# All slot sums on VectorE, and the dense blocks' weights split a pair of blocks ahead

## The chip, the cores and the metric

The kernel runs on one core of a Trainium2 chip. The metric is the time of one execution on the device in microseconds (us); several runs are taken, and their median is compared. The engines are TensorE (PE in the profile, with PEld for its weight loads), VectorE (DVE), ScalarE (ACT), GpSimd (POOL) and SyncE (SP), which issues most transfers. Each engine works through its own queue in order.

## What is computed

One layer, on 2048 tokens of width 512: `x + attention(xn) + experts(xn)`, where `xn` is the layer norm of `x`.

```python
# attention: 32 heads of 16, one shared key and value head
p = softmax(einsum("bhqd,bkd->bhqk", q, k) * Dh ** -0.5)
o = einsum("bhqk,bkd->bhqd", p, v) -> (B, S, 512) @ wo
# experts: 4096 of them, product keys 64 x 64, 32 heads, 2 experts per head and token
s1, s2 = q1 @ k1.T, q2 @ k2.T            # 64 scores each
top 2 of s1, top 2 of s2 -> 4 candidates -> top 2: expert e, gate g = softmax
act = gelu(xn . u[e]);  out = sum over 32 heads, 2 experts of g * act * v[e]
```

## The kernel before, in words

**Two ways for the experts.** The 16 token tiles of 128 form four groups. For groups 0 and 1 the experts are gathered: a *slot* is one expert for each token of a tile, 64 slots per tile, 512 in all. A slot's steps are: an indirect DMA on GpSimd's queue brings 128 rows of u and v (`gather`, L728) into one of 9 buffers (`NGB`); VectorE multiplies u with xn and sums up (`dot`, L740); for each four slots ScalarE makes the tanh of the gelu (`tanh`, L751) and VectorE the weights w (L762, L763); last, the *slot sum* adds w * v to the tile's accumulator (`add`, from L754). Of four slots, VectorE sums three with one instruction each (L772). The fourth is scaled by ScalarE (L769) and added by GpSimd (L770); `adds` (L790) puts it into the list `LATE`, which runs later in the step.

For groups 2 and 3 all 4096 experts are computed, in 32 *blocks* of 128 (`dense`, L558). Before the blocks, *one-hot* batches turn gates and indices into a table of gates (L608 to L636: VectorE L612, L614, L615, TensorE L629). A block's weights come from DRAM (`fetch`, L565, two buffers) and are split into a high and a low part for three-term products (`split`, L584: ScalarE copies the high part, L589, GpSimd subtracts it, L590, once for u and once for v). The parts go into `wk` buffers, of which there are eight (`NWK`); a block takes two. TensorE then makes 12 matmuls (`pact`, L674), ScalarE and VectorE form the gated activations (L692 to L702), and after each odd block `sums` (L646) multiplies the pair of blocks before with its v parts (L656), which VectorE adds up (L659). Block b's gates come by `fetch_gates` (L574).

**The order of the work.** It is written out by hand; each engine's instructions stand in the order in which the program emits them. The main loop makes 256 attention steps and 24 more (`att_steps`, L861). A step emits: the transfers put off in `STORES`; score matmuls (L312) with two exps on ScalarE (L315); the products of the step before's exps with the values (L326); `mid` (L955: tanhs, the activations put off in `ON_ACT` and `BEHIND`, up to four `adds`); two more scores with exps; `LATE`; up to four gathers; and a *filler*. Ahead of each step come as many dots as the count `pos` asks for: 1.65 a step, 2.4 in dense stages.

The filler takes pieces of one long thread (`score_thread`, L834): the experts' scores and top 2 (*items*, L453 to L465) of all groups, and behind group 2's and group 3's items their one-hot batches and dense blocks. Each piece yields its cost in units (`UNIT` for a matmul), and `FILL` sets how many units the loop spends by its last step, the same share in each. At the start of the loop 16.7 units are spent. So the stages are, in this order: items, one-hot, dense blocks, items, one-hot, dense blocks, tail.

Of the kernel before, what the change touches and what calls it, by code (L numbers as in the profile page):

```python
# [16 lines left out]
AF = mybir.ActivationFunctionType  # L17
OP = mybir.AluOpType
# [23 lines left out]
NWK = 8  # L42
NIDX = 10
GS = 8192.0
FILL = 925.0
SCALE = DH ** -0.5
LIMIT2 = 25000.0
C_IN = 0.7978845608028654
C_CUB = 0.044715 * C_IN
POOL_EACH = 4  # L50
UNIT = 0.235


# [1 line left out]
def tile_kernel(ctx, tc, x, wq, wkv, wo, wqT, kT, uv, ub, vb, out):  # L55
    nc = tc.nc
# [47 lines left out]
    for j in range(4):  # L104
        v = blk_f[:, 8 * j:8 * j + 8]
# [452 lines left out]
    def dense(DG, after):  # L558
# [6 lines left out]
        def fetch(b):  # L565
            if b < NB and b not in raws:
                rw = big.tile([P, 2, 512], F32, name="rw", tag="wqt", bufs=2)
                nc.sync.dma_start(rw[:, 0, :], ub[b])
                nc.sync.dma_start(rw[:, 1, :], vb[b])
                raws[b] = rw  # L570
# [13 lines left out]
        def split(b):  # L584
            if b < NB:
                rw = raws.pop(b)
                us, vs = wk_tile(), wk_tile()
                for i, w in enumerate((us, vs)):
                    nc.scalar.copy(w[:, 0, :], rw[:, i, :])  # L589
                    nc.gpsimd.tensor_tensor(out=w[:, 1, :], in0=rw[:, i, :], in1=w[:, 0, :], op=OP.subtract)  # L590
                splits[b] = us, vs
# [29 lines left out]
        for q in range(512 // TB):  # L621
            t0, ql = q // 4 * 64, q % 4
            if ql == 0:
                st = [late[0].tile([P, 16, 64], F32, name="gst", tag="wd", bufs=4) for _ in range(2)]
            onehot(q + 1)
            oa, ob = OH.pop(q)
            p = xtile("pg")
            for i in range(TB):
                nc.tensor.matmul(p[:, i * NB:(i + 1) * NB], oa[:, :, i], ob[:, :, i], start=True, stop=True)  # L629
            pv_ = p.rearrange("p (t b) -> p b t", b=NB)  # L630
            for hb in range(2):
                nc.scalar.copy(st[hb][:, :, ql * TB:(ql + 1) * TB], pv_[:, 16 * hb:16 * hb + 16, :])
            if ql == 3:
                for hb in range(2):
                    store(lambda t0=t0, hb=hb, st=st: nc.sync.dma_start(
                        d_g[16 * hb:16 * hb + 16, :, t0:t0 + 64].rearrange("b p t -> p b t"), st[hb]))  # L636
            yield 1.4
        for j in range(2):
            da = big.tile([P, 2, D], F32, name="da", tag="da", bufs=2)
            for i in range(2):  # L640
# [21 lines left out]
        stt = nc.vector.scalar_tensor_tensor  # L662
        dense_on[0] = 1
        split(0)
        store(lambda: fetch(2))
        run(STORES)
        fetch_gates(0)
        for b in range(NB):
            us, vs = splits.pop(b)
            p = xtile("pact")  # L670
            n = 0
            for k in range(KC):
                for a, c in TERMS:
                    nc.tensor.matmul(p, us[:, a, k * P:(k + 1) * P], XT[DG][k][:, c, :],  # L674
                                     start=n == 0, stop=n == 11)
                    n += 1
                if k == 0:
                    split(b + 1)
                    store(lambda b=b: fetch(b + 3))
                    store(lambda b=b: fetch_gates(b + 1))  # L680
                if k == KC - 1 and b == NB - 1 and after is not None:
                    wp_read(after, range(2))
                if b == NB - 1 and after is not None:
                    load_phase2_xt(SEQ[after][0], k)
                if k < KC - 1:
                    yield 3 * UNIT
            wd = late[0].tile([P, 2, 512], F32R, name="wd", tag="wd", bufs=4)
            if b not in gates:
                run(STORES)
            gy = gates.pop(b)  # L690
            g, y = gy[:, 0, :], gy[:, 1, :]
            nc.scalar.activation(y, p, AF.Square, scale=C_CUB ** 0.5)  # L692
            stt(g, g, 1.0 / GS, p, op0=OP.mult, op1=OP.mult)  # L693
            stt(y, y, C_IN, p, op0=OP.add, op1=OP.mult)  # L694

            def gate(y=y, g=g, wd=wd):
                stt(wd[:, 0, :], y, 1.0, g, op0=OP.add, op1=OP.mult)
                stt(y, y, 1.0, g, op0=OP.add, op1=OP.mult)
                nc.vector.tensor_tensor(out=wd[:, 1, :], in0=y, in1=wd[:, 0, :], op=OP.subtract)
                formed[0] += 1  # L700

            on_act(lambda y=y: nc.scalar.activation(y, y, AF.Tanh))  # L702
            behind(gate)
            held.append((wd, vs))
            yield 3 * UNIT
            if b % 2:
                if ready:
                    yield from sums()
                ready, held = held, []
# [44 lines left out]
    def add(m):  # L754
        ph, c, ti, s = slots[m]
        n, i = divmod(m, SB)
        if i == 0:
            a, th = ACTS.pop(n), TH.pop(n)
            s0 = s
            ga = small.tile([P, SB], F32, name="ga", bufs=3)  # L760
            w = small.tile([P, SB], F32, name="w", bufs=3)
            nc.vector.tensor_mul(ga, a, G[ph, c, ti][:, s0:s0 + SB])  # L762
            nc.vector.scalar_tensor_tensor(w, th, 1.0, ga, op0=OP.add, op1=OP.mult)  # L763
            WT[n] = w
        w = WT[n]
        acc = ACC[TPH * ph + ti]
        v = UV.pop(m)[:, D:]
        if m % POOL_EACH == POOL_EACH - 1:
            nc.scalar.activation(v, v, AF.Copy, scale=w[:, i:i + 1])  # L769
            nc.gpsimd.tensor_tensor(out=acc, in0=acc, in1=v, op=OP.add)  # L770
        else:
            nc.vector.scalar_tensor_tensor(acc, v, w[:, i:i + 1], acc, op0=OP.mult, op1=OP.add)  # L772
        if c == NC - 1 and s == NEG - 1:
            experts_out(TPH * ph + ti)

# [13 lines left out]

    def adds(most):  # L790
        while a_next[0] < a_ready[0] and most > 0:
            m = a_next[0]
            if m % POOL_EACH == POOL_EACH - 1:
                LATE.append(lambda m=m: add(m))
            else:
                add(m)
            a_next[0] += 1
            most -= 1

# [3 lines left out]
            a_ready[0] += SB  # L803


    ON_ACT, BEHIND, LATE, STORES = [], [], [], []
    store = STORES.append
    on_act, behind = ON_ACT.append, BEHIND.append

    def run(fns):  # L810
        todo = fns[:]
        fns.clear()
        for fn in todo:
            fn()
# [44 lines left out]


    def att_steps(d, mid, fill):  # L861
        i = 2 * d
        run(STORES)
        if i < STEPS:
            u, kc = divmod(i, 16)
            if i == 0:
                load_q(0)
            if kc == 4 and u + 1 < 32:
                load_q(u + 1)
            scores(u, kc, 0)  # L870
            scores(u, kc, 1)
        if 0 < i <= STEPS:
            pu, pk = divmod(i - 2, 16)
            pv(pu, pk)
            pv(pu, pk + 1)
            if pk == 14:
                unit_tail(pu)
        mid()
        if i < STEPS:
            scores(u, kc + 1, 0)  # L880
            scores(u, kc + 1, 1)
        run(LATE)
        gathers(4)
        fill()

        if i >= 40 and (i - 40) % 32 == 0 and i - 40 < STEPS:
            pair_tail((i - 40) // 32)
        if i >= 144 and (i - 144) % 128 < 16 and i % 4 == 0:
            qb, j = (i - 144) // 128, (i - 144) % 128 // 4
            block_out(qb, j)  # L890
            spent[0] += 3.6
# [37 lines left out]
    for m in range(0, first, SB):  # L929
        dots(m + SB)  # L930
        tanhs(d_next[0])
        adds(SB)
        run(LATE)
        gathers(SB)
    run(STORES)
    start_stack.close()
# [5 lines left out]
    with tc.manual_schedule(engines={E_.PE, E_.Activation, E_.DVE, E_.Pool, E_.SP}):  # L942
        done0 = spent[0]
        half = STEPS // 2
        pos = float(first)
        for d in range(half + 24):

            if d < half * 3 // 4:
                pos += 2.4 if dense_on[0] else 1.65
            else:  # L950
                pos += max(0.0, NSL - pos) / max(half - 4 - d, 1)
            before = d_next[0]
            dots(int(pos + 0.001))

            def mid():  # L955
                tanhs(before)
                run(ON_ACT)
                run(BEHIND)
                adds(4)

            att_steps(d, mid, lambda: run_scores(until=done0 + (FILL - done0) * (d + 1) / half if d < half else 1e6))
        flush()
        run(STORES)
        while a_next[0] < NSL:
            dots(NSL)
            tanhs(d_next[0])
            adds(SB)
            run(LATE)
            run(STORES)
            gathers(NGB)  # L970
        run(STORES)
# [37 lines left out]
```

## Time and profile before

| | |
|---|---|
| median of 3 runs | 2504.38 us (2497.44 to 2505.39) |
| the profiled execution | 2493.88 us |
| its span, first to last instruction | 2492.2 us |
| mean granted TensorE clock | 0.892 of full speed |
| TensorE / VectorE / ScalarE / GpSimd busy | 83% / 74% / 54% / 35% |
| moved by DMA | 492 MB, 197 GB/s |

Busy shares are means over all stages, which have different limits; so a stage is read by itself, in a table of busy time over stretches of the span. In such a table each engine's busy time stands with its count of instructions (x), then the granted clock. In lists of waits, a row reads: engine and line that waited, `<-` who ended the wait, and then the total in us, the times, and the longest. In rows by group, after the bar: busy us, mean ns of one, idle us just before, and what ended most of it. In timelines: start, duration, engine, line and operation, and in brackets the idle time before it.

### The profile page before, as it was taken

The numbers are of one execution on the slowest core, as the hardware profiler recorded it, in microseconds if no ns is written. First come the engines' busy times: TensorE is split into PE (matmuls) and PEld (weight loads), VectorE is DVE, ScalarE is ACT, GpSimd is POOL, SyncE is SP. The second block draws the span as 40 slices with busy tenths as digits, with TensorE's granted clock in tenths as the row PEclk, the third lists the DMA queues.
The fourth block names the chain that finished last, engine by engine and source line by source line (L and its number), as shares of the span: only waits on it lengthen the run. The fifth ranks groups of instructions, "written<-read, shape, count | busy, mean of one in ns | idle before, by whom it ended". The sixth has DMA issues, their size and how long they took to land. (4 is left out here: it accounts for less than half of the span.)

```text
span 2492.2 us, 35439 instructions
## 1 busy us (share of the span) xinstructions
PE 2057.3 (83%) x10990; PEld 1080.3 (43%) x10990; DVE 1852.4 (74%) x6555; ACT 1346.9 (54%) x1830; POOL 877.5 (35%) x798
## 2 busy tenths in 40 slices
PE   5969898999967778877788899997877887877775
PEld 3624444555533444444444455554434344444431
DVE  5548687979985858877678579999758578777662
ACT  2346565655645665555555556564655565555552
POOL 2013222223223244545444333232234445444430
PEclk8979999999988889988888999998769889888887
DMA  5766666766635575556466677663675656555551
GB/s 191 278 227 220 212 235 224 257 223 218 232 120 157 153 216 181 198 176 196 158 210 208 234 270 247 231 201 128 179 206 187 195 189 196 183 169 181 183 176 53
DMA packets 236099, 492.00 MB, mean 197 GB/s; under 512 B 90736, under 2 KB 90736, under 8 KB 235904
## 3 DMA queue, kind: packets, MB, share of 16 engines
q0 software_dynamic: 73728, 268.47, 31.9%
q1 hardware_dynamic: 159504, 218.17, 27.4%
q10 hardware_dynamic: 2672, 3.05, 0.4%
q8 instruction: 88, 1.44, 0.2%
q14 instruction: 107, 0.88, 0.1%
HBM read 422.18 MB, written 58.20 MB: 193 GB/s over the span
## 5 line engine op out<-in xcount | busy, mean ns | idle before, releaser
L315 ACT ACTIVATE pt<-sc 128x1024 f32<-128x1024 f32 x1024 | 1012.7, 1023 | 528.1 <-PE sc L312 444.3
L770 POOL TENSOR_TENSOR xa<-xa,g 128x512 f32<-128x512 f32 x128 | 172.0, 1344 | 1295.4 <-ACT g L769 441.6
L728 POOL DMA_INDIRECT g<-in_uv_dram,idx x512 | 528.2, 1032 | 258.6 <-issue 99.4
L740 DVE CUSTOM_DVE_ANT_0 junk<-g,xa 128x512 bf16<-128x512 f32 x512 | 458.3, 895 | 155.0 <-DMA g<-in_uv_dram,idx 147.3
L312 PE MATMUL sc<-qa,kaug 64*128 64x512 f32 x2048 | 452.5, 501 | 131.2 <-ACT pt L315 117.9
L326 PE MATMUL pv<-pt,vaug 128*32 128x512 f32 x4096 | 544.9, 653 | 0.0
L312 PEld LDWEIGHTS sc<-qa,kaug 64*128 64x128 f32 x2048 | 185.2, 198 | 527.7 <-ACT pt L315 390.1
L453 PE MATMUL psc<-wk,xt 128*128 128x512 f32 x1536 | 386.0, 402 | 13.1 <-DMA xt<-dxt 5.7
L674 PE MATMUL pact<-xt,wk 128*128 128x512 f32 x768 | 244.3, 468 | 111.3 <-POOL wk L590 98.6
L453 PEld LDWEIGHTS psc<-wk,xt 128*128 128x128 f32 x1536 | 281.8, 189 | 97.5 <-issue 26.5
L772 DVE SCALAR_TENSOR_TENSOR xa<-g,w,xa 128x512 f32<-128x512 f32 x384 | 288.7, 752 | 18.3
L674 PEld LDWEIGHTS pact<-xt,wk 128*128 128x128 f32 x768 | 165.2, 225 | 177.2 <-POOL wk L590 110.4
L326 PEld LDWEIGHTS pv<-pt,vaug 128*32 128x32 f32 x4096 | 113.2, 116 | 281.5 <-issue 279.9
L769 ACT ACTIVATE g<-g,w 128x512 f32<-128x512 f32 x128 | 92.7, 724 | 247.6 <-DVE w L763 218.2
L656 PE MATMUL pout<-wk,wd 128*128 128x512 f32 x768 | 212.3, 428 | 12.8 <-DVE gy L694 10.3
L465 DVE FIND_INDEX8 i<-m,psc 128x8 uint32<-128x64 f32 x1024 | 206.3, 221 | 0.0
L463 DVE MAX8 m<-psc 128x8 f32<-128x64 f32 x1024 | 146.1, 214 | 50.6 <-PE psc L453 50.4
L656 PEld LDWEIGHTS pout<-wk,wd 128*128 128x128 f32 x768 | 154.6, 207 | 59.8 <-DVE gy L694 14.3
L590 POOL TENSOR_TENSOR wk<-rw,wk 128x512 fp32r<-128x512 f32 x128 | 160.7, 1286 | 9.4 <-ACT wk L589 8.7
L629 PE MATMUL pg<-oh 128*128 128x32 f16 x1024 | 74.7, 247 | 58.6 <-DVE oh L615 58.6
L693 DVE SCALAR_TENSOR_TENSOR gy<-gy,pact 128x512 f32<-128x512 f32 x64 | 43.7, 682 | 76.3 <-DMA gy<-dg 51.9
L629 PEld LDWEIGHTS <-oh 128*128 128x128 f16 x1024 | 70.5, 161 | 67.4 <-DVE oh L612 36.0
(146 smaller groups left out, 1584.8 us busy)
## 6 DMA issues: line engine op xcount, KB each, us to landing
wk<-dw SPq DMA_DIRECT2D x96, 512.0 KB
wqt<-in_wqT_dram SPq DMA_DIRECT2D x32, 512.0 KB
dw<-wk SPq DMA_DIRECT2D x32, 512.0 KB
rw<-in_ub_dram SPq DMA_DIRECT2D x64, 256.0 KB
rw<-in_vb_dram SPq DMA_DIRECT2D x64, 256.0 KB
dg<-gst SPq DMA_DIRECT2D x32, 512.0 KB
gy<-dg SPq DMA_DIRECT2D x64, 256.0 KB
g<-in_uv_dram,idx POOLq DMA_INDIRECT x512, 6.0
```

The source lines that it names most:

```text
L312: nc.tensor.matmul(p[:, b, :], kaug[o:o + 64, kc * P:(kc + 1) * P], QA[u][o:o + 64, i, :], start=True, stop=True)
L315: nc.scalar.activation(pt, p, AF.Exp, scale=SCALE)
L326: nc.tensor.matmul(PV[u][32 * j:32 * j + 32, :], vaug[:, kc, :], pt[:, b, :], start=kc == 0, stop=kc == 15)
L453: nc.tensor.matmul(p, XT[g][k][:, a, j * P:(j + 1) * P], WC[n_][k][:, bb, :], start=n == 0, stop=n == 11)
L465: nc.vector.max_index(i8[:, jb, s, :], m8[:, jb, s, :], p[:, s * E:(s + 1) * E])
L590: nc.gpsimd.tensor_tensor(out=w[:, 1, :], in0=rw[:, i, :], in1=w[:, 0, :], op=OP.subtract)
L656: nc.tensor.matmul(p, wd[:, a, j * P:(j + 1) * P], vs[:, c, :], start=n == 0, stop=n == 5)
L674: nc.tensor.matmul(p, us[:, a, k * P:(k + 1) * P], XT[DG][k][:, c, :], start=n == 0, stop=n == 11)
L728: nc.gpsimd.indirect_dma_start(out=gt, out_offset=None, in_=uv, in_offset=bass.IndirectOffsetOnAxis(ap=IDX[ph, c, ti][:, s:s + 1], axis=0))
L740: nc.vector.tensor_tensor_reduce(junk, UV[m][:, :D], XN[TPH * ph + ti], scale=1.0, scalar=0.0, op0=OP.mult, op1=OP.add, accum_out=a[:, i:i ...
L770: nc.gpsimd.tensor_tensor(out=acc, in0=acc, in1=v, op=OP.add)
L772: nc.vector.scalar_tensor_tensor(acc, v, w[:, i:i + 1], acc, op0=OP.mult, op1=OP.add)
```

## The change

GpSimd's branch in `add` goes, and with it `POOL_EACH`, the list `LATE` and ScalarE's scaling: VectorE makes all 512 slot sums. The four gathers of a step move from behind the second scores into `mid`, right behind `adds`. In the dense stage two blocks are split before the first block (one before); blocks b + 2 are split from block b, for even b behind its first matmuls, for odd b at its end, ahead of the pair's `sums`; the fetch into the buffer just read is of block b + 4, and follows each split. For even b the gates' transfer goes ahead of the weights'. A one-hot batch is charged 1.8 units in place of 1.4, and `FILL` grows from 925 to 950.

```diff
-FILL = 925.0
+FILL = 950.0
-POOL_EACH = 4
...
-            yield 1.4
+            yield 1.8
...
         split(0)
+        split(1)
         store(lambda: fetch(2))
+        store(lambda: fetch(3))
...
                 if k == 0:
-                    split(b + 1)
-                    store(lambda b=b: fetch(b + 3))
                     store(lambda b=b: fetch_gates(b + 1))
+                    if b % 2 == 0:
+                        split(b + 2)
+                        store(lambda b=b: fetch(b + 4))
...
             if b % 2:
+                split(b + 2)
+                store(lambda b=b: fetch(b + 4))
                 if ready:
                     yield from sums()
...
-        if m % POOL_EACH == POOL_EACH - 1:
-            nc.scalar.activation(v, v, AF.Copy, scale=w[:, i:i + 1])
-            nc.gpsimd.tensor_tensor(out=acc, in0=acc, in1=v, op=OP.add)
-        else:
-            nc.vector.scalar_tensor_tensor(acc, v, w[:, i:i + 1], acc, op0=OP.mult, op1=OP.add)
+        nc.vector.scalar_tensor_tensor(acc, v, w[:, i:i + 1], acc, op0=OP.mult, op1=OP.add)
...
-            m = a_next[0]
-            if m % POOL_EACH == POOL_EACH - 1:
-                LATE.append(lambda m=m: add(m))
-            else:
-                add(m)
+            add(a_next[0])
...
             scores(u, kc + 1, 1)
-        run(LATE)
-        gathers(4)
         fill()
...
                 run(BEHIND)
                 adds(4)
+                gathers(4)
```

More of the change, by code (lines that the diff above doesn't have):

```diff
@@ L803, in tanhs @@
             a_ready[0] += SB
-    ON_ACT, BEHIND, LATE, STORES = [], [], [], []
+    ON_ACT, BEHIND, STORES = [], [], []
     store = STORES.append
@@ L932, in tile_kernel @@
         adds(SB)
-        run(LATE)
         gathers(SB)
@@ L967, in tile_kernel @@
             adds(SB)
-            run(LATE)
             run(STORES)
```

## The prediction

> **What bounds the kernel now.** I read the page's engine totals and slices first, then the busy table by stage, then the waits of the dense stages, then the timeline.
>
> ```profile
> PE 2057.3 (83%) x10990; PEld 1080.3 (43%) x10990; DVE 1852.4 (74%) x6555; ACT 1346.9 (54%) x1830; POOL 877.5 (35%) x798
> ...
> PE   5969898999967778877788899997877887877775
> ...
> DVE  5548687979985858877678579999758578777662
> ...
> PEclk8979999999988889988888999998769889888887
> ```
>
> No engine is full over the whole span. TensorE (PE) is nearly full in slices 5 to 11 and 23 to 27 only; between them it is at 7 or 8, and its clock digit falls there too. So stages must be taken apart. I cut at the first and last one-hot matmuls (L629) and dense matmuls (L674):
>
> ```profile
> core 0: us, PE busy (x) PEld busy (x) DVE busy (x) ACT busy (x) POOL busy (x), PEclk, DMA share, GB/s
> 151.00:742.00 591.00, 528.64 (x2893) 272.25 (x2892) 474.86 (x2721) 330.06 (x408) 161.82 (x154) 0.94 0.64 220
> 742.00:909.00 167.00, 130.83 (x955) 66.03 (x951) 106.47 (x200) 95.48 (x154) 52.80 (x40) 0.82 0.61 170
> 909.00:1440.00 531.00, 432.57 (x2082) 229.31 (x2080) 403.46 (x748) 298.33 (x407) 246.25 (x220) 0.89 0.60 197
> 1440.00:1733.00 293.00, 274.52 (x1543) 150.90 (x1543) 270.01 (x1656) 173.06 (x212) 87.02 (x82) 0.97 0.64 219
> 1733.00:1871.00 138.00, 107.29 (x823) 55.68 (x823) 93.20 (x179) 78.49 (x135) 43.55 (x35) 0.71 0.63 179
> 1871.00:2435.00 564.00, 443.75 (x2161) 227.40 (x2153) 409.27 (x763) 313.15 (x427) 258.45 (x229) 0.88 0.56 183
> 2435.00:2493.00 58.00, 36.62 (x124) 12.17 (x124) 12.23 (x14) 16.40 (x19) 2.54 (x2) 0.76 0.15 46
> ```
>
> Rows in order: items (72 attention steps by the pace in the code), one-hot (17), dense (54), items (39), one-hot (13), dense (57), tail; 151 us come before. The second item stage is full: 274.5 of 293 on PE, 270.0 on VectorE (DVE), clock 0.97. The two dense stages, 1095 us, are not: PE is idle for 218.7 us (1095 less 876.3) and VectorE for 282.3 (1095 less 812.7). What PE lacks there, first stage, then second:
>
> ```profile
> ACT g L769 <- DVE w L763: 102.4, 28, 7.9
> DVE junk L740 <- DMA g<-in_uv_dram,idx: 65.8, 20, 6.3
> PE sc L312 <- ACT pt L315: 43.3, 41, 4.4
> PE pact L674 <- POOL wk L590: 35.4, 9, 7.1
> DVE gy L693 <- DMA gy<-dg: 27.5, 4, 14.6
> ```
>
> ```profile
> ACT g L769 <- DVE w L763: 110.1, 31, 8.6
> DVE junk L740 <- DMA g<-in_uv_dram,idx: 72.8, 32, 6.0
> PE sc L312 <- ACT pt L315: 51.5, 40, 6.1
> PE pact L674 <- POOL wk L590: 51.2, 12, 8.1
> DVE gy L693 <- DMA gy<-dg: 24.4, 3, 15.1
> ```
>
> Two waits make up 181.4 of PE's 218.7 us: for the exp that frees a score buffer (94.8) and for the split weights (86.6). The timeline of one step shows both causes:
>
> ```profile
> 1099.47 0.16 DVE L763 SCALAR_TENSOR_TENSOR w<-gth,ga 128x4 f32<-128x4 f32 x1
> 1099.67 0.72 ACT L769 ACTIVATE g<-g,w 128x512 f32<-128x512 f32 x1 [4.79 <-DVE w L763]
> ...
> 1100.30 1.12 ACT L589 CAST wk<-rw 128x512 fp32r<-128x512 f32 x2
> ...
> 1102.39 0.50 PE L312 MATMUL sc<-qa,kaug 64*128 64x512 f32 x2 [2.00 <-ACT pt L315]
> ...
> 1108.65 5.96 DVE L740 CUSTOM_DVE_ANT_0 junk<-g,xa 128x512 bf16<-128x512 f32 x1
> 1109.10 4.95 POOL L590 TENSOR_TENSOR wk<-rw,wk 128x512 fp32r<-128x512 f32 x4
> 1110.42 3.18 PE L674 MATMUL pact<-xt,wk 128*128 128x512 f32 x7 [3.17 <-POOL wk L590]
> ```
>
> First, ScalarE stands 4.79 us before the scaling (L769) that it does for GpSimd's sums, because VectorE has not made the weights w; the exps queue behind it, and PE stands behind the exps. Second, the subtraction (L590) comes out just as the block needs it. Third, a dot (L740) lasts 5.96 us beside four subtractions.
>
> **The change, part by part.**
>
> ```profile
> L770 POOL TENSOR_TENSOR xa<-xa,g 128x512 f32<-128x512 f32 x128 | 172.0, 1344 | 1295.4 <-ACT g L769 441.6
> ...
> L772 DVE SCALAR_TENSOR_TENSOR xa<-g,w,xa 128x512 f32<-128x512 f32 x384 | 288.7, 752 | 18.3
> ...
> L769 ACT ACTIVATE g<-g,w 128x512 f32<-128x512 f32 x128 | 92.7, 724 | 247.6 <-DVE w L763 218.2
> ...
> L590 POOL TENSOR_TENSOR wk<-rw,wk 128x512 fp32r<-128x512 f32 x128 | 160.7, 1286 | 9.4 <-ACT wk L589 8.7
> ```
>
> *Sums.* GpSimd loses 128 x 1.344 = 172 us, ScalarE 128 x 0.724 = 93 us and its 218 us of standing before them; VectorE gains 128 x 0.752 = 96 us. Per step: 1.65 slots in item and one-hot stages, a quarter of them moved, 0.31 us; 2.4 in dense stages, 0.45 us. The gathers, now issued right after VectorE's sums, no longer queue on GpSimd behind L770. Each still waits there for the sum that frees its slot, with subtractions queued behind it; those are now over two steps ahead of their use, so up to some 15 us of that costs TensorE nothing.
>
> *Splits.* Nothing is added: 128 copies, 128 subtractions and the same weight transfers. The split of an odd block stood 2.1 code units ahead of its use, less than a step; every split now stands at least 8.5 ahead, over two steps, and two splits no longer follow within one step. The gates' transfer stands ahead of the weights' on SP for even blocks, so it does not wait there for a subtraction. The weights' transfer waits on SP for its buffer's two subtractions, as before, with the attention's loads behind it.
>
> *Pace.* The step's filler goes from (925 - 16.7)/256 = 3.55 units to (950 - 16.7)/256 = 3.65; a one-hot batch is charged 1.8 for 1.4, so 2.53 batches a step become 2.03. By this pace the stages take 70, 20, 51, 40, 16 and 55 steps.
>
> *Items.* The moved sums fall on an engine that is nearly full in the second stage: VectorE 270.0/39 = 6.92 us a step, plus 0.31, plus some 0.11 for denser items, is 7.34, over PE's 7.04 + 0.10. The step of 7.51 grows by between 0.10 (pace alone) and 0.42 (all of it on the path); I take 0.29, nearer to the full engine: 40 x 7.80 = 312. In the first stage VectorE has room (6.60 of 8.21): 70 x 8.36 = 585.
>
> *One-hot.*
>
> ```profile
> L612 DVE TENSOR_TENSOR oh<-oh 128x2048 f16<-128x2048 f16 x29 | 36.5, 1257 | 3.5 <-PE pg L629 3.5
> ...
> L614 DVE TENSOR_TENSOR oh<-oh 128x512 f16<-128x512 f16 x29 | 17.5, 602 | 0.0
> ...
> L615 DVE TENSOR_TENSOR oh<-oh 128x512 f16<-128x512 f16 x30 | 12.7, 424 | 1.0
> ```
>
> A batch costs VectorE 2.28 us; half a batch less per step saves 1.16, the sums add 0.31. 9.82 and 10.62 us a step become 8.97 and 9.77: 20 x 8.97 + 16 x 9.77 = 335 us for 305 before. If VectorE does not set these steps, nothing is saved: 366.
>
> *Dense.* With ScalarE free of w and weights ready, most of the 181 us of PE idle goes, and what is late next is VectorE. Its work: 812.7, plus 67 sums (a third of 96 + 104 by its own count in the two windows is what GpSimd made) x 0.752 = 50. Blocking of dots by L590 is worth this much in the first dense stage, against an item stage:
>
> ```profile
> L740 DVE CUSTOM_DVE_ANT_0 junk<-g,xa 128x512 bf16<-128x512 f32 x130 | 152.2, 1171 | 67.0 <-DMA g<-in_uv_dram,idx 65.8
> ```
>
> ```profile
> L740 DVE CUSTOM_DVE_ANT_0 junk<-g,xa 128x512 bf16<-128x512 f32 x64 | 43.6, 681 | 3.5 <-DMA g<-in_uv_dram,idx 2.9
> ```
>
> That is 130 x 0.49 = 64 us. All subtractions stay, but runs of four become mostly runs of two. Bounds for both stages: no relief, or all of about 100; I take 25. Five fewer steps take 20 us of slot work along: 812.7 + 50 - 25 - 20 = 818. VectorE's idle of 282: waits for gathers 139 to 60, since they leave GpSimd some microseconds earlier; gates 52 to 30; the other 91 to 47, since most of it is waiting for a late ScalarE. The start of each dense stage now splits three blocks at once with two weight buffers, where ScalarE may stand for one transfer, which no row of before shows: between 0 and the longest transfer wait above, 15.1; I take 5 for each stage, as the block's own matmuls cover part. Together 147 (bounds: 18 of unavoidable small gaps, and 282). Dense: 818 + 147 = 965 us, 9.1 a step for 9.86.
>
> The Trainium skill ("SBUF — State Buffer", "Who interferes with whom") says that a VectorE instruction with two SBUF inputs and a GpSimd instruction that reads SBUF lock each other out, whoever comes first. The 5.96 us dot agrees. By that rule the moved sums, with two SBUF inputs, can be locked out too; this case's sums never were:
>
> ```profile
> L772 DVE SCALAR_TENSOR_TENSOR xa<-g,w,xa x384: 746/752/756, 146.4 to 2439.5; 128x512 f32<-128x512 f32 x192
> ```
>
> **Sum.** 151 + 585 + 335 + 965 + 312 + 58 = 2406, against a span of 2492.2; with the 1.7 us around it 2407.7, against the profiled 2493.88. The median of the runs, 2504.38, is 1.0042 times that: **2418**.
>
> **Rivals.**
> *VectorE becomes the bound (slower).* The moved sums lie wholly on the path and its idle does not shrink, since each dot still waits for its gather and for subtractions. For it: VectorE is at 92% in the second item stage, and dots wait 139 us for gathers. Against it: those gathers queued behind L770. Price: dense 862.8 + 282.3 - 20 = 1125, items 597 and 317: 2583 + 1.7, times 1.0042 = 2596. The point: other stages make 1441, so it decides from (2492.2 - 1441)/106 = 9.92 us a dense step on. The Trainium skill ("Perfetto Trace Analysis", "Optimizing Scalar/DVE Operations") speaks for this rival: when VectorE is saturated it advises to offload work from it, the reverse of this change.
> *VectorE never waits.* All PE idle and clock loss in dense goes; dense is VectorE's 818 + 18 = 836. 2279 x 1.0042 = 2288. Against it: gather and gate transfers keep some latency.
> *The early split doesn't come early.* There are eight wk buffers; in the built program's waits 17 splits now make ScalarE wait for the sums' matmuls (L656) just ahead, where before it waited for none. Exps queue behind it. At most one step's filler each, 3.65 of the code's units, which are about a microsecond of PE (items: 3.55 units in steps that PE fills): 17 x 3.6 = 61 us, and 2469 x 1.0042 = 2479. Against it: PE runs its filler in that time.
>
> **How the numbers follow.** Forecast 0.70, VectorE never waits 0.08, ScalarE waits for buffers 0.10, VectorE bound 0.12. The range runs from dense at 8.4 us a step (890) to 9.8 (1040), which covers the third rival and half the way to the others: 2340 to 2495. 0.3% is about what a measurement of this kernel can tell from no change. Faster: 0.68 + 0.08 + 0.07 = 0.83; same 0.03; slower 0.12 + 0.02 = 0.14.
>
> **What would show it.** Right: no ScalarE wait for w; waits of pact for L590 under 15 us and of sc for exps under half in the dense stages; PE clock there at 0.92 or more; VectorE's busy time near 1920; its wait for gathers under 80; second item stage at 7.6 to 7.9 us a step with VectorE over PE. Wrong: dense steps over 9.9 us; dots whose mean in dense stays at 1.2 us; new waits of L589 on L656 with exps behind; item stages over 8 us.

## The result, and the profile after

The changed kernel takes 2382.2 us (median of 4 runs, 2380.30 to 2383.65); beside it the kernel before took 2504.89 us. The ratio is 0.9507, with a 95% interval of 0.9471 to 0.9542: 4.9% faster. The profiled execution's span went from 2492.2 to 2379.1 us. The first line of its page:

```profile
PE 2019.6 (85%) x10990; PEld 1064.9 (45%) x10990; DVE 1928.2 (81%) x6683; ACT 1274.4 (54%) x1702; POOL 767.9 (32%) x670
```

The table of busy time by stage, cut in the same way as before (items, one-hot, dense, items, one-hot, dense, tail; 152 us come ahead):

```profile
core 0: us, PE busy (x) PEld busy (x) DVE busy (x) ACT busy (x) POOL busy (x), PEclk, DMA share, GB/s
152.00:724.00 572.00, 520.68 (x2827) 268.66 (x2828) 487.58 (x2733) 304.01 (x368) 132.53 (x119) 0.95 0.65 223
724.00:903.00 179.00, 145.17 (x1040) 70.44 (x1038) 113.90 (x229) 103.50 (x163) 46.25 (x37) 0.79 0.60 169
903.00:1366.00 463.00, 393.08 (x2002) 213.07 (x2002) 406.93 (x724) 270.43 (x363) 213.43 (x181) 0.93 0.66 217
1366.00:1677.00 311.00, 285.35 (x1580) 154.39 (x1575) 284.24 (x1704) 166.43 (x200) 76.95 (x69) 0.97 0.62 213
1677.00:1825.00 148.00, 115.71 (x894) 59.18 (x894) 107.35 (x214) 86.65 (x143) 46.03 (x37) 0.75 0.71 196
1825.00:2319.00 494.00, 418.93 (x2096) 220.68 (x2088) 428.43 (x776) 286.62 (x383) 227.83 (x191) 0.92 0.63 202
2319.00:2379.00 60.00, 38.77 (x142) 12.73 (x142) 15.58 (x25) 16.29 (x18) 0.00 (x0) 0.77 0.21 69
```

| stage | before us | forecast | after us |
|---|---|---|---|
| items, first | 591 | 585 | 572 |
| one-hot, both | 305 | 335 | 327 |
| dense, both | 1095 | 965 | 957 |
| items, second | 293 | 312 | 311 |
| ahead of the loop, and tail | 209 | 209 | 212 |

By these cuts the dense stages are 138 us shorter and the first items 19, and 40 us are given back in the one-hot and the second item stages. The cuts do not all lie at the matmuls that the prediction names, though. The last matmul of the second dense stage's sums ends 30 us ahead of the cut before (2405 for 2435) and 11 ahead after (2308 for 2319). From the first dense matmul to the last matmul of the sums, the two dense stages take 1073 us before and 961 after, 112 less, and what follows the second one takes 87 and 71. The dense stages hold the gain by either count. In them VectorE is now busy for 835 of 957 us and TensorE's clock rose from 0.88 and 0.89 to 0.92 and 0.93. The waits of the first dense stage, then of the second:

```profile
PE pout L655 <- DVE gy L696: 44.9, 12, 8.2
...
DVE junk L744 <- DMA g<-in_uv_dram,idx: 17.4, 14, 5.7
DVE gy L695 <- DMA gy<-dg: 17.2, 1, 17.2
...
PE sc L311 <- ACT pt L314: 6.3, 11, 0.8
...
PE pact L675 <- POOL wk L589: 1.4, 1, 1.4
```

```profile
PE pout L655 <- DVE gy L696: 26.8, 11, 4.3
DVE junk L744 <- DMA g<-in_uv_dram,idx: 25.8, 17, 3.4
...
PE sc L311 <- ACT pt L314: 16.7, 24, 3.6
PE pact L675 <- DVE da L658: 14.8, 7, 3.6
```

Every wait that was named is down: the dots' wait for gathers from 139 to 43 us, TensorE's for exps from 95 to 23, its wait for GpSimd's subtraction (now L589) from 87 to 1. What TensorE waits for now is VectorE: its gated activations (L696) and its sums (L658). What did not fall is the time in which GpSimd's subtractions hold VectorE up. Groups of the whole run, before and then after (after the bar: busy us, mean ns):

```profile
L740 DVE CUSTOM_DVE_ANT_0 junk<-g,xa 128x512 bf16<-128x512 f32 x512 | 458.3, 895 | 155.0 <-DMA g<-in_uv_dram,idx 147.3 <-DVEq L255 3.0
...
L744 DVE SCALAR_TENSOR_TENSOR gq<-act 128x4 f32<-128x4 f32 x128 | 26.7, 209 | 4.4
...
L746 DVE SCALAR_TENSOR_TENSOR gy<-gq,act 128x4 f32<-128x4 f32 x128 | 20.8, 162 | 4.3
```

```profile
L744 DVE CUSTOM_DVE_ANT_0 junk<-g,xa 128x512 bf16<-128x512 f32 x512 | 410.3, 801 | 56.3 <-DMA g<-in_uv_dram,idx 47.3 <-DVEq L254 3.3
...
L750 DVE SCALAR_TENSOR_TENSOR gy<-gq,act 128x4 f32<-128x4 f32 x128 | 44.1, 345 | 4.3
...
L748 DVE SCALAR_TENSOR_TENSOR gq<-act 128x4 f32<-128x4 f32 x128 | 40.0, 313 | 4.4
```

The dots lost 512 x 0.094 = 48 us of it, but the two small instructions behind them, of four elements each, took up 128 x (0.104 + 0.183) = 37 us. Counted for every VectorE instruction from the first to the last dense matmul of each stage, as what it took over a short one of its group (the tenth percentile), the time held up is 132 us before and 130 after.

### The profile page after: what moved, and what is told of

It reads as the page before. It is cut to its first block, busy times and chain, and to the rows that moved or that the text cites. A ratio compares the mean times of both kernels' runs of the same rounds, so it can differ in the third digit from the quotient of the medians.

```text
span 2379.1 us, 35223 instructions
## 1 busy us (share of the span) xinstructions
PE 2019.6 (85%) x10990; PEld 1064.9 (45%) x10990; DVE 1928.2 (81%) x6683; ACT 1274.4 (54%) x1702; POOL 767.9 (32%) x670
## 4 chain that ended last, share of the span: by engine, by line
DVE 28%; PE 27%; issue 21%; POOL 9%; DMA 6%; ACT 2%; SPq 1%; POOLq 0%; DVEq 0%; ACTq 0%
PE pv L325 8%; PE psc L452 6%; DVE xa L772 6%; PE sc L311 6%; POOL g L732 5%; DVE i L464 5%; DVE junk L744 4%; POOL wk L589 4%; DVE m L462 3%; DMA g<-in_uv_dram,idx 2%; PE pwo L360 2%; ACT pt L314 2%; PE pout L655 2%; PE pact L675 1%; DVE rsb L349 1%
## 5 line engine op out<-in xcount | busy, mean ns | idle before, releaser
L732 POOL DMA_INDIRECT g<-in_uv_dram,idx x512 | 584.9, 1142 | 1506.2 <-DVE xa L772 1295.0
L311 PE MATMUL sc<-qa,kaug 64*128 64x512 f32 x2048 | 441.6, 492 | 57.2 <-ACT pt L314 44.5
L744 DVE CUSTOM_DVE_ANT_0 junk<-g,xa 128x512 bf16<-128x512 f32 x512 | 410.3, 801 | 56.3 <-DMA g<-in_uv_dram,idx 47.3
L772 DVE SCALAR_TENSOR_TENSOR xa<-g,w,xa 128x512 f32<-128x512 f32 x512 | 385.0, 752 | 18.5 <-DVE w L767 0.6
L655 PE MATMUL pout<-wk,wd 128*128 128x512 f32 x768 | 224.1, 443 | 87.6 <-DVE gy L696 71.6
L675 PE MATMUL pact<-xt,wk 128*128 128x512 f32 x768 | 215.9, 430 | 33.3 <-DVE da L658 18.5
L675 PEld LDWEIGHTS pact<-xt,wk 128*128 128x128 f32 x768 | 152.1, 205 | 84.2 <-DVE da L658 22.6
L589 POOL TENSOR_TENSOR wk<-rw,wk 128x512 fp32r<-128x512 f32 x128 | 166.3, 1328 | 40.4 <-ACT wk L588 32.8
L704 ACT ACTIVATE gy<-gy 128x512 f32<-128x512 f32 x64 | 40.3, 631 | 132.7 <-DVE gy L696 132.0
L588 ACT CAST wk<-rw 128x512 fp32r<-128x512 f32 x128 | 74.0, 629 | 35.7 <-PE pout L655 21.0
L658 DVE TENSOR_TENSOR da<-da,pout 128x512 f32<-128x512 f32 x128 | 82.2, 679 | 5.4 <-PE pout L655 5.4
```

What stands on the lines that cost most here:

```text
L311: nc.tensor.matmul(p[:, b, :], kaug[o:o + 64, kc * P:(kc + 1) * P], QA[u][o:o + 64, i, :], start=True, stop=True)
L655: nc.tensor.matmul(p, wd[:, a, j * P:(j + 1) * P], vs[:, c, :], start=n == 0, stop=n == 5)
L732: nc.gpsimd.indirect_dma_start(out=gt, out_offset=None, in_=uv, in_offset=bass.IndirectOffsetOnAxis(ap=IDX[ph, c, ti][:, s:s + 1], axis=0))
L744: nc.vector.tensor_tensor_reduce(junk, UV[m][:, :D], XN[TPH * ph + ti], scale=1.0, scalar=0.0, op0=OP.mult, op1=OP.add, accum_out=a[:, i:i ...
```

## The experiments

Two theories stood after the result. **A**, from the prediction's reading of the dense stages: what cost time were two heads of queues, ScalarE's stand before the scaling (which holds the exps) and the late split. **B**: what counts is that GpSimd has less to do. **C**, that the pace did it, was tried as well. When A fell, **F** took its place: VectorE bounds the dense stages already before the change, and loses time because its dots wait for gathers that queue behind GpSimd's sum. As it was first put, F also said why the gathers are late: GpSimd's sum waits for ScalarE. Three expectations use the letters otherwise: for the gathers late in the step, B stands for "the place of the gathers counts", and for the split subtracted by VectorE and the fill, A stands for VectorE as the bound, which is F's first half. Each ratio is against the kernel before, run on the same chip, with its 95% interval. The table holds, for the two stretches from the first to the last dense matmul, times added up: their length, VectorE's busy and idle time, and three waits.

| kernel | time us | ratio (interval) | length | VectorE busy, idle | dots for gathers | scores for exps | pact for GpSimd |
|---|---|---|---|---|---|---|---|
| before | - | 1 | 1003 | 745, 258 | 108 | 83 | 99 |
| changed | 2382 | 0.9507 (0.9471 to 0.9542) | 886 | 770, 116 | 27 | 16 | 5 |
| sums alone | 2390 | 0.9571 (0.9515 to 0.9627) | 911 | 767, 144 | 26 | 12 | 63 |
| splits alone | 2453 | 0.9827 (0.9770 to 0.9883) | 959 | 733, 226 | 114 | 128 | 14 |
| pace alone | 2511 | 1.0064 (1.0040 to 1.0087) | 1016 | 736, 280 | 124 | 79 | 99 |
| sums and splits | 2378 | 0.9526 (0.9473 to 0.9578) | 894 | 782, 112 | 25 | 19 | 10 |
| scaling kept on ScalarE | 2398 | 0.9594 (0.9569 to 0.9619) | 883 | 767, 116 | 30 | 79 | 2 |
| split subtracted by VectorE | 2329 | 0.9331 (0.9302 to 0.9359) | 836 | 726, 110 | 29 | 26 | 0 |
| gathers late in the step | 2379 | 0.9517 (0.9494 to 0.9541) | 884 | 770, 114 | 30 | 15 | 6 |
| fill in place of subtraction | 2295 | 0.9177 (0.9137 to 0.9216) | 800 | 648, 152 | 62 | 13 | 3 |
| gathers ahead of GpSimd's sum | 2441 | 0.9785 (0.9759 to 0.9810) | 955 | 764, 191 | 32 | 62 | 73 |
| VectorE subtracts, sums kept | 2421 | 0.9704 (0.9683 to 0.9725) | 926 | 714, 212 | 126 | 114 | 0 |
| no scaling | 2492 | 0.9984 (0.9963 to 1.0005) | 1002 | 744, 258 | 115 | 10 | 139 |
| gathers behind the splits | 2383 | 0.9560 (0.9523 to 0.9596) | 895 | 748, 147 | 73 | 23 | 1 |

Length and busy time are read off the table of busy time by stretch, whose last row adds the two stretches up, here before and then after; the waits are sums over the instructions that start in them:

```profile
sum 1003.00, PE 793.27 PEld 420.74 DVE 745.04 ACT 557.70 POOL 483.78; mean PE 396.64 PEld 210.37 DVE 372.52 ACT 278.85 POOL 241.89
```

```profile
sum 886.00, PE 752.04 PEld 406.33 DVE 769.97 ACT 515.86 POOL 426.59; mean PE 376.02 PEld 203.16 DVE 384.99 ACT 257.93 POOL 213.29
```

### The parts by themselves

*Sums alone.* The diff of `add`, `adds`, `LATE` and the gathers, as in the change; `split`, `fetch`, 1.4 and 925 as before.

> Before with the first part of the change alone: VectorE makes all slot sums and the gathers follow them; splits and pace stay as they were. Theory A (two queue heads: ScalarE stands before the scaling for w and holds the exps, and the split comes late): the first head is gone, the second stays: about 2430 us (2405 to 2455), the waits of pact for L590 at 80 us or more, no wait of ScalarE for w. Theory B (what counts is that GpSimd has less to do and gathers come sooner): nearly all of the gain, 2385 to 2405. Theory C (the pace does it): 2480 to 2505.

*Splits alone.* The diff of the dense stage's `split` and `fetch` as in the change, nothing else.

> Before with the second part alone: the weights are split a pair of blocks ahead; GpSimd still makes every fourth sum, pace as before. Theory A: pact no longer waits for L590, ScalarE still stands some 200 us before the scaling: about 2455 us (2430 to 2475). Theory B: 2485 to 2505. Theory C: 2490 to 2505.

*Pace alone.*

```diff
-FILL = 925.0
+FILL = 950.0
...
-            yield 1.4
+            yield 1.8
```

> Before with the third part alone: a one-hot batch is charged 1.8 units and FILL is 950. Theories A and B: 2485 to 2510. Theory C: 2390 to 2420.

*Sums and splits, old pace:* the changed kernel with these two lines put back.

> The changed kernel without the pace: sums on VectorE and early splits, a one-hot batch at 1.4 units and FILL 925. Theory A: 2380 to 2400, the two gains together. Theory B: the same as the sums alone within 10 us. Theory C: 2480 to 2505.

The sums alone bring 4.3% of the 4.9, the splits alone 1.7% (A's number), the pace alone costs 0.6%, and the pace on top of the other two can't be told from nothing. C is out. The parts don't add up: 4.3 and 1.7 would be 6.0, and the two together bring 4.7. The sums' share is B's number, not A's, though with them TensorE still waits for the late split in the whole run:

```profile
PE pact L673 <- POOL wk L589: 63.1, 21, 6.2
```

So 63 us of waits of TensorE stand in a kernel that is almost as fast as the changed one, in which they are gone: taking them away on top is worth at most some 1% (the two intervals overlap). In the kernel before, however, the late split does cost something. With the splits alone, the dense stretches are 44 us shorter, while in the whole run the dots wait as long as before (147 us) and TensorE's wait of 99 us for the split is nearly gone:

```profile
DVE junk L745 <- DMA g<-in_uv_dram,idx: 153.7, 54, 6.6
...
PE pact L676 <- POOL wk L590: 13.7, 3, 6.0
```

B had expected nothing there (2485 to 2505, measured 2453). Some of it may be the gates' transfer, which the same edit moves ahead on SP: VectorE's wait for it falls from 52 to 33 us in the stretches. So TensorE's wait for the split is a part of what the dense stages lose, and the smaller one beside the sums' 92 us (1003 to 911).

### ScalarE's stand, put back and taken away

*Scaling kept on ScalarE.* The kernel before with the splits and the pace of the change, and one more line:

```diff
-            nc.gpsimd.tensor_tensor(out=acc, in0=acc, in1=v, op=OP.add)
+            nc.vector.tensor_tensor(out=acc, in0=acc, in1=v, op=OP.add)
```

> Early splits and the new pace, and no sum on GpSimd; but every fourth slot is still scaled by ScalarE where it was before, and VectorE (not GpSimd) adds it there, with the gathers behind it. GpSimd is relieved as in the changed kernel, ScalarE still waits for w. Theory A: ScalarE stands some 150 us or more before the scaling, and most of the sums' share of the gain is lost: 2425 to 2460 us. Theory B (GpSimd's load): as the changed kernel within 15 us, 2370 to 2397.

*No scaling.* The kernel before without ScalarE's part of GpSimd's sums:

```diff
-            nc.scalar.activation(v, v, AF.Copy, scale=w[:, i:i + 1])
```

> Before with ScalarE's scaling left out, so that GpSimd adds unscaled rows (the fourth slots' weights are missing from the output). GpSimd's sum still comes behind VectorE's sums of the same accumulator, so it still comes after w. Theory A and theory F: ScalarE no longer stands, GpSimd's sum and the gathers behind it come sooner: 2430 to 2465; F adds that the dots' wait for gathers falls in step, to under 80 us. Theory B (GpSimd's load alone): 2485 to 2505.

Whole-run waits: before, then with the scaling kept, then with no scaling.

```profile
ACT g L769 <- DVE w L763: 218.2, 62, 8.6
...
DVE junk L740 <- DMA g<-in_uv_dram,idx: 147.3, 56, 6.3
PE sc L312 <- ACT pt L315: 117.9, 108, 6.1
...
PE pact L674 <- POOL wk L590: 98.6, 23, 8.1
```

```profile
ACT g L774 <- DVE w L768: 206.1, 84, 6.0
...
PE sc L312 <- ACT pt L315: 115.7, 137, 4.4
...
DVE junk L745 <- DMA g<-in_uv_dram,idx: 45.8, 36, 6.1
```

```profile
DVE junk L740 <- DMA g<-in_uv_dram,idx: 154.8, 56, 6.4
...
PE pact L674 <- POOL wk L590: 138.5, 23, 10.2
...
PE sc L312 <- ACT pt L315: 42.7, 49, 5.5
```

Read the second fence against the first: ScalarE stands 206 us and TensorE waits 116 us for exps, as before, and yet the kernel is only 0.9% off the changed one (0.9594 for 0.9507), and its dense stretches are no longer (883 for 886). The third is the mirror: ScalarE's stand is gone, TensorE's wait for exps falls by 75 us, and nothing is gained (0.9984); in the dense stretches TensorE waits 40 us more for the split weights instead, and some 50 more for VectorE's results (28 to 81, before L656, L361 and L674). The first half of A, ScalarE's stand, is refuted in both directions; its second half, the late split, is the splits' share above. Both runs lie at B's numbers, the first 1 us outside them (2398 for 2370 to 2397): GpSimd's 128 sums cost as much without the scaling as with it, and moved off GpSimd they cost little. F's reason is refuted with A: without the scaling, the dots' wait for gathers was to fall to under 80 us and the time to 2430 to 2465, and neither came (155 us in the whole run, and 2492). But the wait itself, about 150 us in the first fence and the third, is 46 in the second, whose kernel is fast. So what is left of F is that the gathers come late for another reason.

### Where the gathers stand

*Gathers ahead of GpSimd's sum.* The kernel before, with one line added in `mid`:

```diff
                 adds(4)
+                gathers(3)
```

> Before with one edit: three of a step's four gathers, whose buffers VectorE's sums have freed, are issued right behind those sums, ahead of GpSimd's own sum; the fourth follows it. Nothing else changes: ScalarE scales, GpSimd adds and splits as before. Theory F (VectorE bounds the dense stages, and what it loses is its dots' wait for gathers that queue behind GpSimd's sum, which waits for ScalarE): the dots' wait in the dense stages falls from 117 us to under 70, and 15 to 45 us of time go: 2455 to 2485. Theory A (ScalarE's stands count) and theory B (GpSimd's load counts): within 10 us of before.

*Gathers late in the step.* The changed kernel, `gathers(4)` moved from `mid` to behind the second scores, ahead of `fill()`.

> The changed kernel with the step's four gathers back behind the second pair of scores. The order on GpSimd's queue is the same, since nothing stands between; Theory A: within 8 us of the changed kernel. Theory B (the place of the gathers counts): 10 to 30 us slower.

*Gathers behind the splits.* The changed kernel, `gathers(4)` moved behind `fill()`.

> The changed kernel with the step's four gathers behind the filler, so that in the steps that split weights they queue on GpSimd behind subtractions that wait for ScalarE's copies. No sum goes back to GpSimd. Theory F (a gather late in GpSimd's queue holds up VectorE, which bounds the dense stages): the dots' wait in the dense stages rises from 31 us to 60 or more, and the kernel is 10 to 40 us slower, 2390 to 2422. Rival (the gain came from VectorE's sums themselves, and the place of a gather matters little now): within 8 us of the changed kernel.

The first one leaves GpSimd all its work and ScalarE its stand (166 us), and gains 2.15%, half of what the sums bring, where A and B expected nothing (within 10 us); in the whole run:

```profile
ACT g L769 <- DVE w L763: 165.9, 62, 7.4
...
DVE junk L740 <- DMA g<-in_uv_dram,idx: 48.2, 26, 4.1
```

F's wait fell as expected (the whole run had 147 us), and the time came out 14 us under F's range. How early is enough can be seen in the timelines. Before, one group of sums with what follows it on GpSimd's queue, and then after:

```profile
1099.74 2.33 DVE L772 SCALAR_TENSOR_TENSOR xa<-g,w,xa 128x512 f32<-128x512 f32 x3
...
1102.20 1.28 POOL L770 TENSOR_TENSOR xa<-xa,g 128x512 f32<-128x512 f32 x1 [3.25 <-ACT wk L589]
...
1103.62 1.24 POOL L728 DMA_INDIRECT g<-in_uv_dram,idx  x1
```

```profile
1021.58 3.11 DVE L772 SCALAR_TENSOR_TENSOR xa<-g,w,xa 128x512 f32<-128x512 f32 x4
1022.60 1.35 POOL L732 DMA_INDIRECT g<-in_uv_dram,idx  x1 [11.48 <-DVE xa L772]
1024.26 1.25 POOL L732 DMA_INDIRECT g<-in_uv_dram,idx  x1 [0.30 <-DVE xa L772]
1025.81 0.94 POOL L732 DMA_INDIRECT g<-in_uv_dram,idx  x1 [0.30 <-issue]
...
1027.40 3.70 DVE L744 CUSTOM_DVE_ANT_0 junk<-g,xa 128x512 bf16<-128x512 f32 x1
1028.01 2.52 POOL L589 TENSOR_TENSOR wk<-rw,wk 128x512 fp32r<-128x512 f32 x2
```

Before, the first gather comes 3.9 us after the first sum begins (1103.62 less 1099.74); after, 1.0 us. The medians over all such groups of the dense stretches, worked out in the same way, are 3.9 before and 1.0 after; with no scaling 3.8, with the gathers ahead 1.0. So it is not ScalarE's lateness that delays the gathers: VectorE's three sums and GpSimd's own one stand in front of them in any case, and 2.9 us decide whether the dots find their rows.

Moving the gathers within the step changes nothing (0.9517), as no other instruction of GpSimd stands between. Behind the splits, the dots' wait comes back in good part, 27 to 73 us, but by the ratios the kernel is slower by 0.5% only, about 13 us, which is F's lower end, and the two intervals overlap. The table suggests why it is so little: VectorE's idle time is up by 31 us, but its busy time is down by 22. A dot in the stretches takes 0.79 us on average, for 0.95 in the changed kernel and 0.69 where GpSimd subtracts nothing: more of them meet GpSimd at its gathers and not at subtractions. F's wait is confirmed and its price here is not shown, as the two effects nearly cancel.

### What the subtractions cost VectorE

*Split subtracted by VectorE,* in the changed kernel; *VectorE subtracts, sums kept* is the same line in the kernel before:

```diff
-                    nc.gpsimd.tensor_tensor(out=w[:, 1, :], in0=rw[:, i, :], in1=w[:, 0, :], op=OP.subtract)
+                    nc.vector.tensor_tensor(out=w[:, 1, :], in0=rw[:, i, :], in1=w[:, 0, :], op=OP.subtract)
```

> The changed kernel with the low part of each split subtracted by VectorE; GpSimd does nothing but gathers in the main loop. Theory A (VectorE bounds the dense stages, and GpSimd's subtractions hold up its instructions with two SBUF inputs for some 120 us): 120 us of blocking go and 128 x 0.70 = 90 us of work come: faster by 15 to 40 us, 2342 to 2367, and no dot over 0.9 us. Rival (the blocked time lay in VectorE's slack): VectorE has 90 us more to do: 2410 to 2470.

> Before with the subtraction of each split on VectorE, issued as late as before; GpSimd keeps its 128 sums. GpSimd is relieved of 161 us, about what the change took from it with the sums (172). Theory B (GpSimd's load): most of the gain, 2390 to 2425. Theory F: 118 us of blocking on VectorE go, 90 us of work come, and the dots still wait for gathers behind the sums: 2460 to 2490, the waits of dots over 90 us in the dense stages.

*Fill in place of subtraction,* in the changed kernel:

```diff
-                    nc.gpsimd.tensor_tensor(out=w[:, 1, :], in0=rw[:, i, :], in1=w[:, 0, :], op=OP.subtract)
+                    nc.gpsimd.memset(raw(w[:, 1, :]), 0.0)
```

> The changed kernel with GpSimd filling the low part of the split weights with zeros in place of the subtraction, so that the low part of the dense weights is left out. GpSimd's instruction then reads nothing. Theory A: no dot of VectorE is held up, the dense stages lose 100 us or more of VectorE time until TensorE bounds them: 2280 to 2320 us. Rival (the blocked time lay in slack): 2370 to 2395.

The dots of the changed kernel, of the one that subtracts on VectorE, and of the one that fills (ns minimum/median/maximum):

```profile
L744 DVE CUSTOM_DVE_ANT_0 junk<-g,xa x512: 664/685/6166, 137.8 to 2321.7; 128x512 bf16<-128x512 f32 x171
```

```profile
L744 DVE CUSTOM_DVE_ANT_0 junk<-g,xa x512: 670/686/750, 137.7 to 2272.9; 128x512 bf16<-128x512 f32 x171
```

```profile
L744 DVE CUSTOM_DVE_ANT_0 junk<-g,xa x512: 668/686/742, 138.0 to 2235.9; 128x512 bf16<-128x512 f32 x171
```

In the two kernels without a subtraction on GpSimd no dot lasts over 0.75 us. With the fill, VectorE's busy time in the dense stretches falls by 122 us (770 to 648) and their length by 86 (2295 us, inside the 2280 to 2320 expected): most of the blocked time lay on the path. The fill also takes 128 x (1.33 - 0.54) = 101 us of work off GpSimd, but that did not bring the gathers sooner to the dots, which wait 62 us for them, for 27. With the subtraction on VectorE, 83 us of work are added:

```profile
L589 DVE TENSOR_TENSOR wk<-rw,wk 128x512 fp32r<-128x512 f32 x128 | 83.2, 692 | 21.7 <-ACT wk L588 21.7
```

and still VectorE's busy time falls by 44 us and the stretches by 50. Of the kernels that leave nothing out this is the fastest: 2329.47 us, ratio 0.9331, 1.9% below the changed kernel (0.9331/0.9507). The number expected for it (2342 to 2367) was too cautious.

In the kernel before, the same line brings 3.0%, B's number and not F's (2460 to 2490), though the waits are F's (126 us of waits for gathers stay). F had left out that a prompt VectorE also ends the wait for the late split (99 to 0) and, with it, most of the wait for the gates' transfer (52 to 10), which stood on SP behind that of the weights: VectorE's busy time falls by 31 us, near F's 28, but its idle time by 46 as well.

The Trainium skill ("SBUF — State Buffer", "Who interferes with whom") says that a VectorE instruction with two SBUF inputs contends with a GpSimd instruction that reads SBUF, and not with one that only writes it. These runs agree: 6166 ns beside subtractions, 742 beside fills.

## Why the prediction was right, and where its reasons were not

*The sum.* Forecast 2418, measured 2382.2: 36 us too high, of which 13 lie in the first items (585 for 572), 8 in the one-hot stages, 8 in the dense ones, and 3 the other way in the tail; the rest is in the scaling to the median, since the changed kernel's profiled execution lies closer to its median (2379.1 of span to 2382.2) than the one before (2492.2 to 2504.4).

*Items.* Right in number; the split between the terms was not. The second stage came to 311 us for 312, 7.8 us a step, with VectorE busy for 284.2 of 311 and TensorE for 285.4. VectorE had been put above TensorE; it stands level with it. The forecast gave 11 us of the growth to the pace (40 x 7.61 = 304 for 293) and 8 to the moved sums. From the first item matmul behind the dense stage (L453) to the first one-hot matmul (L629), the stage takes 298 us before, 303 with the sums alone, 313 with the pace alone and 313 in the changed kernel: the sums add 5 us by themselves and nothing on top of the pace.

*One-hot and pace.* Right in sign: 305 to 327 for 335. From the first one-hot matmul to the first dense one, the two stages are 33 us longer with the pace alone and 4 shorter with the sums alone, so the moved sums, put at 0.31 us a step, are not seen here either. Pace alone costs 0.6%, and with the rest nothing that can be measured.

*Dense.* Right in size, 957 for 965, and in that VectorE's work and waits add up to it. The cuts flatter it a little: by the matmuls themselves the gain is 112 us, where 130 were forecast (1095 to 965). Two terms were off and cancelled. VectorE's work was put at 818 and is 835: of the 25 us of relief from blocking next to nothing came (132 us to 130), since VectorE's small instructions took over what the dots lost. Its idle time was put at 147 and is 122, as the dots' wait fell to 43 us, not 60.

*The step that failed* is the reading that the 181 us of TensorE's waits, for exps and for split weights, are what the dense stages lose, and that VectorE becomes late only next. For the exps (95 us) the runs refute it: their wait could be put back for 0.9% and taken away for nothing. For the split weights (87 us) it holds in part: the early splits alone bring 1.7%, but with the sums moved, a wait of 63 us for the weights could stay for 0.6%, which the intervals can't tell from nothing. What the runs showed in its place is the gathers: three of four issued earlier, and nothing else, bring 2.15%. VectorE's idle time fell by 142 us (258 to 116) in the stretches that became 117 us shorter, and 81 of the 142 are dots that no longer wait for gathers. So VectorE's waits counted before the change already. That VectorE alone set these stages is not shown, as the early splits gained 44 us while the dots waited as long as before. The prediction's sum had the gathers' term, and as the largest of VectorE's idle time (139 to 60); so its number came from VectorE's side, while its text named TensorE's waits as the loss. TensorE's wait for the exps looks, for the most part, like the same delay seen from an engine further down; no run takes the two apart.

*The slower rival* was wrong in its condition: VectorE did become fuller, but its idle time shrank by far more than the moved sums added. *The rival of the early split's buffers* is seen and small: ScalarE waits 21 us in all for the sums' matmuls, 12 times. *VectorE never waits* (2288) did not come: VectorE still stands 122 of the 957 us, and 43 of them are dots that wait for gathers.

*Open:* the gathers' place accounts for half of what the sums bring (2.15 of 4.3%). The rest was not taken apart. Between the kernel with the gathers ahead and the one with the sums alone, VectorE's wait for the gates' transfer falls from 39 to 4 us in the stretches, and the time in which its instructions are held up, counted as above, from 153 to 114; its waits for ScalarE do not fall (60 and 66). That later gathers cost in the changed kernel what F says is not shown either, because in that run the blocking fell in turn.

## What to carry to other kernels

A wait on the busiest engine is not yet a loss: before crediting its removal, ask which engine's chain closes the loop through the stage, and try to put the wait back by itself. Where one queue both starts transfers and computes, whatever computes there delays the transfers, and a few microseconds can decide whether their reader stands. Work moved onto a busier engine can pay if it removes what that engine waits for, and a helper engine that locks it out can cost more than it helps.

## What the runs showed of the hardware

A VectorE instruction that meets GpSimd's subtractions can wait for a whole run of them, not for one: a dot of 0.685 us lasted 6.17 us. It began 0.60 us ahead of the first of four subtractions that followed each other, and ended 0.55 us behind the last (the changed kernel):

```profile
1159.01 6.17 DVE L744 CUSTOM_DVE_ANT_0 junk<-g,xa 128x512 bf16<-128x512 f32 x1
1159.61 5.01 POOL L589 TENSOR_TENSOR wk<-rw,wk 128x512 fp32r<-128x512 f32 x4
```

It also hits small instructions, of four elements in each of 128 partitions: the mean of one group (`gy` from `gq` and `act`) went from 162 ns before to 345 after, and it is 162 again where GpSimd fills instead. And GpSimd's fill of the same tile, which reads nothing, takes 0.54 us for the subtraction's 1.33 and held up no dot:

```profile
L589 POOL MEMSET wk<- 128x512 f32 x128 | 63.8, 542 | 17.7 <-PE pact L675 10.6 <-PE pout L655 7.1
```
